# Two attention blocks on one core: where the first row maxima are split, when the k stacks are loaded, and where the reciprocals' spread stands in SP's queue

## Chip, core, metric

One NeuronCore of a Trainium2 chip. The metric is the device time of one execution in microseconds (us); before the change it is 1768.89, the median of three runs (1768.71 to 1769.63).

## What is computed

Two independent attention blocks over x of 2048 x 640 with 32 heads of 20, all in float32; their outputs stand side by side.

```python
# A: each position sees 8 keys, 2 apart
logits = einsum("bhsd,bhswd->bhsw", q, kg) * scale     # kg, vg: k, v at pos - 0, 2, .. 14
attn = softmax(where(mask, logits, -1e9)); o = einsum("bhsw,bhswd->bhsd", attn, vg)
# B: full attention
p = softmax(einsum("bhqd,bhkd->bhqk", q, k) * DH ** -0.5)
o = einsum("bhqk,bhkd->bhqd", p, v)
out = concat([oA @ woA, oB @ woB], axis=-1)            # q, k, v = x @ wqkv for both
```

## The kernel before, in words

Float32 factors are split into a high part that TensorE's fp32r can hold and the low rest, and a product is made of three passes (`PASSES`) or of stacked rows.

Stages: first A's projections, whose rows go to DRAM (`qa_d`, `ka_d`, `va_d`); then B's q and k projections, which go to DRAM as `qb_d` and `kb_d`; then B's v rows (30 groups of matmuls, `v_group`, `ve` to `vb_d`), beside which the row maxima of B's first 24 steps are made; then the main loop. Block A's attention runs all along on POOL (`a_scores`, `a_values`, tiles `akv`, `al`, `am`), a piece every few steps.

The main loop has `NS` = 512 steps. Heads go in 8 groups of 4 (`GH`); a group has 4 units, one for each 512 query columns (`NQC`), and a unit has 16 steps of 128 keys (`NKB`). `stacks[g]` holds the group's k (tile `bk`, loaded by `b_keys`, four transfers from `kb_d`, two buffers in turn) and v (`vb`, `v_piece`); `rings[0]` is the tile `bq` with the queries of four units. For a step PE makes four score tiles (`s_matmul`: rows of k against queries, 62 rows deep, `bq,bk` in the profile), ACT makes exp of each (`e`), and two steps later PE multiplies with v (`b_pv`, `e,vb`). 24 steps ahead (`LEAD`) PE makes the same products the other way round (`m_matmul`, 60 rows, `bk,bq`), and DVE reduces them to row maxima (`mx`).

The maximum enters the scores as two more rows of the query tile. `max_rows` does it once a unit: `turn` (DVE: last reduction and transpose into `mtr`), `parts` (split into a high and a low part), `store` (four DMAs `mdr<-mtr`), `load` (two DMAs `bq<-mdr`). The unit's first score matmul waits for the first of those loads.

`normalize` ends a unit: the sums, row `DH` of each head in `raw` (`braw`), go by DRAM into `sm` (`s_d<-braw`, `sm<-s_d`), `turn` takes their reciprocals on DVE and stores them (`s_d<-sm`), `bcast` spreads them over partitions (four DMAs `rb<-s_d`), POOL multiplies (`braw<-braw,rb`), and `out` stores `ot_b`.

What sets the order: every engine runs its instructions in the order in which the program names them (`InOrder`). `after(n, fn)` puts fn n steps ahead, `tick` runs what is due; a list of functions of one step runs in the order in which they were asked for. DVE work that must not stand anywhere is put in `beside` and comes at a mark `G` in the unit's table (`UNIT`, `UNIT_V`, `flush`). All loads and nearly all stores are issued by SP, whose queue is one line: an issue that has to wait holds up every later one. Each issue also waits for the landing of the DMA eight before it (eight semaphores in turn). The bank of the eight-bank tile `ps_st` is picked by `one` and `two` in the loop, before it by `bank` (0 to 3) and `wide` (pairs 4-5 and 6-7 in turn).

Of the kernel before, what the change touches and what calls it, by code (L numbers as in the profile page):

```python
# [9 lines left out]
F32 = mybir.dt.float32  # L10
F32R = mybir.dt.float32r
AF = mybir.ActivationFunctionType
ALU = mybir.AluOpType
# [10 lines left out]
NG = H // GH  # L24
# [16 lines left out]
NKB = 16  # L41
UP = 12
NS = NG * NQC * NKB
LEAD = 24
# [21 lines left out]
def attention_pair(ctx, tc, xa, wqk_a, wv_a, wo_a, xb, wqk_b, wv_b, wo_b, oa, ob):  # L66
# [6 lines left out]
    pe, gp, sp = (InOrder(tc, e) for e in (nc.tensor, nc.gpsimd, nc.sync))  # L73
    dve, act = InOrder(tc, nc.vector, 0.075, 960), InOrder(tc, nc.scalar, 0.111, 1400)


    now = [0]
    due = {}

    def after(n, fn, *args):  # L80
        due.setdefault(now[0] + n, []).append((fn, args))

    loop = [None]
    beside = []

    def small(us, op, *args):

        t = dve.us
        op(*args)
        dve.us = t + us  # L90
# [13 lines left out]
    def tick():  # L104
        now[0] += 1
        for fn, args in due.pop(now[0], ()):
            fn(*args)
# [93 lines left out]
    def x_pieces(x, n, second=None, at=()):  # L201

        t = columns(*at or (n,))
        src = x[:, n * 512:(n + 1) * 512].rearrange("(k p) c -> p k c", p=128)

        def piece(a, b):
            u = t[a // (KC - 1)]
            m = a % (KC - 1)
            split(u[:, 0, m:m + b - a], u[:, 1, m:m + b - a], src[:, a:b], "p", second)
        return t, [lambda a=a, b=b: piece(a, b) for a, b in PAIRS]  # L210
# [390 lines left out]
    def v_piece(g, b0, b1):  # L601

        sp.dma_start(stacks[g][1][:, b0:b1], vb_d[b0 * 128:b1 * 128, g * GH * VC:g * GH * VC + VG]
                     .rearrange("(b p) c -> p b c", p=128))
# [51 lines left out]
    def max_rows(m4, m1, q, qc):  # L656

        mt = sb.tile([128, 3, 32], F32R, tag="mtr", bufs=2, name="mtr")
        md = dr.tile([2, GH * 512], F32, tag="mdr", bufs=4, name="mdr")
        raw = mt[:, 0].bitcast(F32)  # L660

        def parts():
            gp.tensor_copy(mt[:, 1], raw)
            gp.tensor_tensor(mt[:, 2], raw, mt[:, 1].bitcast(F32), ALU.subtract)

        def store():
            for b in range(4):
                sp.dma_start(md.rearrange("t (j b c) -> b j t c", b=4, c=32)[b], mt[32 * b:32 * b + 16, 1:].bitcast(F32))

        def load():  # L670
            for r in range(2):
                sp.dma_start(q[r * HALF + BS:r * HALF + BM, qc].bitcast(F32),
                             md[:, r * 1024:(r + 1) * 1024].rearrange("t (p c) -> t p c", p=2))
        def turn():

            small(0.17, dve.tensor_reduce, m1[:, :16], m4.rearrange("p r a c -> p (r a) c"), AX.X, ALU.max)
            small(0.21, dve.transpose, raw, m1)
            after(1, parts)
            after(2, store)
            after(4, load)  # L680
        if loop[0] is None:
            after(1, turn)
        else:
            beside.append((turn,))

    def normalize(raw, g, c0, t, then):

        sm = sb.tile([128, 16], F32, tag="sm", bufs=2, name="sm")
        s_d = dr.tile([2, GH, 512], F32, tag="s_d", bufs=4, name="s_d")
        rb = sb.tile([128, 512], F32, tag="rb", bufs=2, name="rb")  # L690

        def bcast():
            for j in range(GH):
                sp.dma_start(rb[32 * j:32 * j + 32], s_d[1, j].partition_broadcast(32))

        def out():
            for j in range(GH):
                r0 = (g * GH + j) * DH
                sp.dma_start(ot_b[r0:r0 + DH, c0:c0 + 512], raw[32 * j:32 * j + DH])
        def turn():  # L700

            small(0.24, dve.reciprocal, sm, sm)
            after(1, sp.dma_start, s_d[1].rearrange("j (p c) -> j p c", c=16), sm)
            after(2, bcast)
            after(4, pool, raw, raw, rb, ALU.mult)
            after(8, out)
            if then:
                after(9, then)
        after(t, sp.dma_start, s_d[0], raw[DH:128:32])
        after(t + 1, sp.dma_start, sm, s_d[0].rearrange("j (p c) -> j p c", c=16))  # L710
        if now[0] - loop[0] < NS - LEAD - NKB // 2 - 4:
            after(t + 3, beside.append, (turn,))
        else:
            after(t + 3, turn)
# [32 lines left out]
    def b_max(i):  # L747

        m4 = max_tiles(i)[0]
        pq, ch = divmod(i % NKB, 2)  # L750
        for j in range(2):
            p = wide()
            for r in range(2):
                m_matmul(i, j, r, p[:, r])
            dve.tensor_reduce(m4[:, :, pq, 2 * ch + j], p, AX.X, ALU.max)
        max_end(i)
# [195 lines left out]
    def v_group(n, half, s):  # L952
        p = bank()
        rows15(p, lambda xi, k: chunk(XB[n], xi, k)[:, s % 4 * 128:s % 4 * 128 + 128], WV[half])
        ve = ones[s % 4]
        act.copy(ve[:, :16 * VC].rearrange("p (h c) -> p h c", c=VC)[:, :, :DH],
                 p[:, :320].rearrange("p (h d) -> p h d", d=DH))
        give(p)
        c = 16 * VC + 11 * half
        after(1, sp.dma_start, vb_d[s * 128:(s + 1) * 128, half * 16 * VC:half * 16 * VC + c], ve[:, :c])  # L960
# [29 lines left out]
    def a_load():  # L990

        w = big(2, [128, 2, KC, 320], "wx")
        wt[:] = [w]
        m = rows_a[0][1]
        return [lambda wi=wi, a=a, b=b: sp.dma_start(w[:, wi, a:b].bitcast(F32), wa_d[m, :, wi, a:b])
                for wi in range(2) for a, b in AK]
# [20 lines left out]
    for n, half, s in V_GROUPS[:-LAG]:  # L1017
        v_group(n, half, s)
        tick()
        groups += 1  # L1020
        if q_loads:
            for _ in range(4 if groups == 1 else 1):
                q_loads.pop(0)()
        if groups == 1:
            wait[0] = 5
        if groups in (8, 16):
            XB[groups // 8 - 1], more = x_pieces(xb, groups // 8 - 1, gp, (groups // 8 - 1, groups // 8 + 1))
            for fn in more:
                fn()
        if groups > 6:  # L1030
            for i in islice(steps, 1):
                b_max(i)
        if groups in (9, 11, 15, 17, 19, 23, 25, 28):
            next(a_work, None)
        if groups in (22, 23, 26):
            v_piece(0, *((8, 12), (12, 16), (0, 4))[(groups - 21) // 2])
        if groups in (18, 21):
            a_columns(UP + groups // 21)
        if groups == 24:
            for n, fn in enumerate(a_load()):  # L1040
                after(1 + n, fn)
        if groups == 14:
            a_turn(*done_a.pop(0)[1:])
        turn_parts()
        if groups == 28:
            wait[0] = 2
            load_out(wo_a, WO, (0,))
        if loads and groups >= 28:
            loads.pop(0)()
# [34 lines left out]
    next(steps)  # L1084
    for i in range(NS + LAG):
        g, sub = divmod(i, NQC * NKB)
        if sub == 4 and g + 1 < NG:
            for n, fn in enumerate(b_keys(g + 1)):
                after(1 + n, fn)
            after(33, v_piece, g + 1, 0, NKB)  # L1090
        if i >= NKB and i % NKB in (1, 3, 5, 7) and i // NKB + 3 < NG * NQC:
            b_queries(*divmod(i // NKB + 3, NQC))[i % NKB // 2]()
        if i in (NS - 56, NS - 40):
            out_first((i - NS + 56) // NKB)
        tick()
        if loads and i % 2:
            loads.pop(0)()
        if i > 14 and i % 4 == 3 and next(a_work, 0) == 0:
            for d in done_a:
                d[0] -= 1  # L1100
        if i % NKB == SLOT and done_a and done_a[0][0] <= 0:
            beside.append((lambda d=done_a.pop(0): a_turn(*d[1:]),))
        turn_parts()
        if i == 1:
            load_out(wo_a, WO, (1,))

            spare += [sb.tile([128, 2, 512], F32, tag="last0", bufs=2, name="more") for _ in range(2)]
        if i < NS - LEAD:
            next(steps, None)
            if not left_a[0] and not WO_b:  # L1110
                load_out(wo_b, WO_b)
            continue
        read_at.clear()
        flush()
        if i < NS:
            b_qk(i)
        if i % 2:
            b_pv(i - LAG - 1)
            b_pv(i - LAG)
            if fill:  # L1120
                fill.pop(0)()
# [57 lines left out]
```

## Time and profile before

| | |
|---|---|
| median of three runs | 1768.89 us |
| the profiled execution | 1771.62 us |
| its span, first to last instruction | 1769.8 us |
| busy: PE / DVE / ACT / POOL | 1751.3 / 1345.4 / 1333.0 / 1230.0 us |
| mean granted TensorE clock | 0.999 |
| 425 to 1420 us: busy PE / DVE / ACT / POOL | 986.5 / 951.2 / 915.2 / 864.6 of 995 us |

Rows of the timeline are: start, length in us, engine, line, operation, out<-in, shapes, count; in square brackets the idle time of that engine before it and what ended it. Nearly every row has line L61, that of the recording helper, so tiles tell the place. SPq rows are DMA issues, and their length is the issue, not the transfer. In the chain of waits a row "DMA x" starts at the issue and ends at the landing.

### The profile page before, as it was taken

To read this page: it belongs to the slowest core of one execution; us is meant where nothing else is said; L and a number is where in the kernel's file an instruction comes from. 1 tells how busy PE (TensorE), PEld (TensorE's weight loads), DVE (VectorE), ACT (ScalarE), POOL (GpSimd) and SP (SyncE) were. 2 spreads that over 40 slices of the span, in tenths; PEclk is the share of its full clock that TensorE was granted. 3 is DMA by queue.
4 is the path that set the end of the run, shared out by engine and by line. 5 is a ranking of instruction groups with operands and counts; after the bars stand their busy time and mean duration, and the time that the engine had idled before them with its cause. 6 is when DMAs were issued, how large, how long until landed. Compare 5 with 4: busy or idle time off the path is not lost.

```text
span 1769.8 us, 31997 instructions
## 1 busy us (share of the span) xinstructions
PE 1751.3 (99%) x11331; PEld 999.9 (56%) x11331; DVE 1345.4 (76%) x1819; ACT 1333.0 (75%) x2598; POOL 1230.0 (70%) x1088
## 2 busy tenths in 40 slices
PE   9999999999999999999999999999999999999999
PEld 8988888874454444444444444444444444444569
DVE  3102333679999999999999999999999999999400
ACT  4323222229989999999999999989999999989981
POOL 0000683585988888888989897988888898745442
PEclk9999999999999999999999999999999999999999
DMA  7657867774435554554464455535552534222123
GB/s 259 195 169 244 303 240 262 239 222 125 143 114 151 153 172 126 135 151 134 140 165 148 140 150 158 150 108 154 156 166 90 152 97 130 77 74 62 57 71 115
DMA packets 212152, 269.74 MB, mean 152 GB/s; under 512 B 91676, under 2 KB 131740, under 8 KB 211000
## 3 DMA queue, kind: packets, MB, share of 16 engines
q1 hardware_dynamic: 211416, 267.04, 50.3%
q8 instruction: 89, 1.46, 0.3%
q14 instruction: 71, 0.58, 0.1%
q10 hardware_dynamic: 576, 0.66, 0.1%
HBM read 192.87 MB, written 74.74 MB: 151 GB/s over the span
## 4 chain that ended last, share of the span: by engine, by line
PE 85%; DMA 4%; DVE 4%; POOL 3%; issue 1%; SPq 1%; ACT 1%; DVEq 0%; POOLq 0%; ACTq 0%
PE ps_st L61 85%; DVE mx L61 4%; DMA s_d<-sm 1%; POOL akv L61 1%; SPq L61 1%; DMA bq<-mdr 1%; ACT e L61 1%; DMA bq<-qb_d 1%; POOL xn L61 0%; DMA stg<-wv_b 0%; DMA mdr<-mtr 0%; DMA wx<-wa_d 0%; DMA qb_d<-pr 0%; POOL xl L61 0%; POOL ao L61 0%
## 5 line engine op out<-in xcount | busy, mean ns | idle before, releaser
L61 DVE TENSOR_REDUCE mx<-ps_st 128x1 f32<-128x512 f32 (+1 forms) x1500 | 1219.9, 879 | 83.2 <-PE ps_st L61 74.7
L61 ACT ACTIVATE e<-ps_st 128x512 f32<-128x512 f32 x2048 | 1067.9, 609 | 41.3 <-PE ps_st L61 22.7
L61 PE MATMUL ps_st<-bq,bk 62*128 62x512 f32 x2048 | 612.7, 441 | 6.7 <-DMA bq<-mdr 5.8
L61 PEld LDWEIGHTS ps_st<-bq,bk 62*128 62x128 f32 x2048 | 289.0, 184 | 486.1 <-ACT e L61 352.3
L61 PE MATMUL ps_st<-bk,bq 60*128 60x512 f32 x2048 | 556.2, 434 | 1.6 <-DMA bq<-qb_d 1.2
L61 PE MATMUL ps_st<-e,vb 128*32 128x512 f32 x4096 | 543.0, 604 | 3.1
L61 POOL TENSOR_TENSOR braw<-braw,more 128x512 f32<-128x512 f32 x224 | 288.1, 1286 | 171.1 <-ACT more L61 154.1
L61 POOL TENSOR_TENSOR akv<-akv,aq 128x1280 f32<-128x1280 f32 x64 | 188.5, 2945 | 184.8 <-DVE w L61 184.8
L61 POOL TENSOR_TENSOR akv<-akv 128x640 f32<-128x640 f32 (+3 forms) x304 | 282.6, 930 | 23.8
L61 PEld LDWEIGHTS ps_st<-bk,bq 60*128 60x128 f32 x2048 | 270.1, 184 | 31.5 <-DVE mx L61 10.5
L61 ACT COPY ro<-ps_st 128x320 f32<-128x320 f32 (+2 forms) x132 | 62.5, 475 | 191.8 <-PE ps_st L61 156.9
L61 PEld LDWEIGHTS ps_st<-e,vb 128*32 128x32 f32 x4096 | 82.2, 108 | 159.5 <-issue 73.6
L61 POOL TENSOR_TENSOR akv<-akv,al 128x1280 f32<-128x1280 f32 x64 | 152.1, 2376 | 0.2
L61 ACT COPY more<-ps_st 128x512 f32<-128x512 f32 x224 | 132.4, 591 | 1.6 <-PE ps_st L61 1.4
L61 PE MATMUL ps_st<-ww,xn 128*128 128x320 f32 x768 | 126.6, 315 | 0.0
L61 PEld LDWEIGHTS ps_st<-ww,xn 128*128 128x128 f32 x768 | 114.2, 189 | 20.0 <-ACT e L61 7.5
L61 PE MATMUL ps_st<-xn,w 128*128 128x512 f32 x480 | 117.6, 394 | 0.0
L61 PE MATMUL ps_st<-wc,xn 128*128 128x512 f32 (+1 forms) x432 | 102.0, 382 | 0.0
L61 PEld LDWEIGHTS ps_st<-xn,w 128*128 128x128 f32 x480 | 90.2, 188 | 20.9
L61 ACT CAST pr<-ps_st 128x512 fp32r<-128x512 f32 x40 | 23.5, 587 | 103.6 <-PE ps_st L61 103.6
L61 DVE TENSOR_TENSOR pr<-ps_st,pr 128x512 fp32r<-128x512 f32 x40 | 27.7, 692 | 93.0 <-ACT pr L61 93.0
L61 PEld LDWEIGHTS ps_st<-wc,xn 128*128 128x128 f32 x432 | 80.6, 190 | 13.9
(69 smaller groups left out, 1065.8 us busy)
## 6 DMA issues: line engine op xcount, KB each, us to landing
akv<-ka_d SPq DMA_DIRECT2D x128, 320.0 KB
akv<-va_d SPq DMA_DIRECT2D x128, 320.0 KB
wx<-wa_d SPq DMA_DIRECT2D x24, 480.0 KB
kb_d<-pr SPq DMA_DIRECT2D x20, 512.0 KB
qb_d<-pr SPq DMA_DIRECT2D x20, 512.0 KB
bk<-kb_d SPq DMA_DIRECT2D x16, 640.0 KB
bq<-qb_d SPq DMA_DIRECT2D x64, 160.0 KB
rb<-s_d SPq DMA_DIRECT2D x128, 64.0 KB
```

The costliest lines, as they stand in the source:

```text
L61: return self.tc.keep_in_program_order(op(*a, **k))
```

## The change

Three edits.

1. `parts` takes an engine. Before the loop (`loop[0] is None`, which holds for unit 0's maxima alone) VectorE splits at once, in the step of the transpose; the store comes one step later and the load two, where they were two and four. To this belongs that `wx`, block A's weights for the next rows (four loads, `a_load`), is asked for one step later.
2. In the loop, from group 1 on, the four `b_keys` loads of the next group are issued at steps 2 to 5 of the group and not at 4 to 7. The v piece stays at its step (35 from step 2, 33 from step 4).
3. In `normalize`, for units 0 to 28 (`slow`), `bcast` and the multiplication come one step later.

```diff
-        def parts():
-            gp.tensor_copy(mt[:, 1], raw)
-            gp.tensor_tensor(mt[:, 2], raw, mt[:, 1].bitcast(F32), ALU.subtract)
+        def parts(e=gp):
+            e.tensor_copy(mt[:, 1], raw)
+            e.tensor_tensor(mt[:, 2], raw, mt[:, 1].bitcast(F32), ALU.subtract)
...
             small(0.21, dve.transpose, raw, m1)
+            if loop[0] is None:
+                parts(dve)
+                after(1, store)
+                after(2, load)
+                return
             after(1, parts)
...
-            after(2, bcast)
-            after(4, pool, raw, raw, rb, ALU.mult)
+            after(2 + slow, bcast)
+            after(4 + slow, pool, raw, raw, rb, ALU.mult)
...
-        if now[0] - loop[0] < NS - LEAD - NKB // 2 - 4:
+        slow = now[0] - loop[0] < NS - LEAD - NKB // 2 - 4
+        if slow:
...
-                after(1 + n, fn)
+                after(2 + n, fn)
...
-        if sub == 4 and g + 1 < NG:
+        if sub == (2 if g else 4) and g + 1 < NG:
...
-            after(33, v_piece, g + 1, 0, NKB)
+            after(35 if g else 33, v_piece, g + 1, 0, NKB)
```

SP's queue at the first maxima (stage of the v rows; `stg`, `vb_d`, `vb`, `aq`, `akv` are other loads and stores), before:

```order
L61 DMA vb<-vb_d 128x4x95
L61 DMA vb_d<-ve 128x347
L61 DMA mdr<-mtr 16x2x32 x4
L61 DMA wx<-wa_d 128x960
L61 DMA vb_d<-ve 128x336
L61 DMA aq<-qa_d 128x640
L61 DMA akv<-ka_d 128x640 x2
L61 DMA wx<-wa_d 128x640
L61 DMA vb_d<-ve 128x336
L61 DMA vb<-vb_d 128x4x95
L61 DMA bq<-mdr 2x1024 x2
```

and now:

```order
L61 DMA vb<-vb_d 128x4x95
L61 DMA mdr<-mtr 16x2x32 x4
L61 DMA vb_d<-ve 128x347
L61 DMA bq<-mdr 2x1024 x2
L61 DMA vb_d<-ve 128x336
L61 DMA aq<-qa_d 128x640
L61 DMA akv<-ka_d 128x640 x2
L61 DMA wx<-wa_d 128x960
```

The maxima's store and load moved ahead of one v store, the first `wx` load, and the loads of block A; `wx` moved back.

SP's queue in the first unit of group 1 ( `bk` 40x4096 and 22x4096 are the two pieces of a half k stack), before:

```order
L61 DMA ot_b<-braw 20x512 x4
L61 DMA bq<-qb_d 40x1024
L61 DMA akv<-va_d 128x640 x2
L61 DMA s_d<-braw 4x512
L61 DMA ka_d<-ro 128x320
L61 DMA bk<-kb_d 40x4096
L61 DMA bq<-qb_d 20x1024
L61 DMA sm<-s_d 128x16
L61 DMA bk<-kb_d 22x4096
L61 DMA bk<-kb_d 40x4096
L61 DMA bq<-qb_d 40x1024
L61 DMA bk<-kb_d 22x4096
```

and now:

```order
L61 DMA ot_b<-braw 20x512 x4
L61 DMA bk<-kb_d 40x4096
L61 DMA bq<-qb_d 40x1024
L61 DMA bk<-kb_d 22x4096
L61 DMA akv<-va_d 128x640 x2
L61 DMA s_d<-braw 4x512
L61 DMA bk<-kb_d 40x4096
L61 DMA ka_d<-ro 128x320
L61 DMA bq<-qb_d 20x1024
L61 DMA sm<-s_d 128x16
L61 DMA bk<-kb_d 22x4096
L61 DMA bq<-qb_d 40x1024
```

Three of the four k loads now stand ahead of `ka_d<-ro` (a store that waits for ACT), and two ahead of the sums' store `s_d<-braw`.

SP's queue later in the same unit, at the reciprocals (`s_d<-sm` to the maxima's load), before:

```order
L61 DMA s_d<-sm 128x16
L61 DMA rb<-s_d 32x512 x4
L61 DMA mdr<-mtr 16x2x32 x4
L61 DMA akv<-ka_d 128x640 x2
L61 DMA bq<-mdr 2x1024 x2
```

and now:

```order
L61 DMA s_d<-sm 128x16
L61 DMA mdr<-mtr 16x2x32 x4
L61 DMA akv<-ka_d 128x640 x2
L61 DMA rb<-s_d 32x512 x4
L61 DMA bq<-mdr 2x1024 x2
```

The spread, which reads what `s_d<-sm` wrote, changed places with the maxima's store and two loads of block A; it still stands ahead of `bq<-mdr`. On POOL the multiplication keeps its place but in units 27 and 28, where it falls behind one and two splits.

## The prediction

> **What bounds the kernel now.** I began with the page's first line, then asked who waits for whom on PE.
>
> ```profile
> PE 1751.3 (99%) x11331; PEld 999.9 (56%) x11331; DVE 1345.4 (76%) x1819; ACT 1333.0 (75%) x2598; POOL 1230.0 (70%) x1088
> ...
> PE ps_st L61 <- DMA bq<-mdr: 5.8, 6, 1.9
> ```
>
> PE works 1751.3 of 1769.8 us, so only what it waits for, or what slows it, can be won. Of its waits the largest by far is for the maxima's load into the query tile: 5.8 us in six places. PE's timeline shows them, the idle time in brackets.
>
> ```profile
> 391.40 0.46 PE L61 MATMUL ps_st<-bq,bk 62*128 62x512 f32 x1 [1.92 <-DMA bq<-mdr]
> ...
> 603.02 0.50 PE L61 MATMUL ps_st<-bq,bk 62*128 62x512 f32 x1 [1.10 <-DMA bq<-mdr]
> ...
> 768.45 0.49 PE L61 MATMUL ps_st<-bq,bk 62*128 62x512 f32 x1 [0.49 <-DMA bq<-mdr]
> ...
> 933.94 0.49 PE L61 MATMUL ps_st<-bq,bk 62*128 62x512 f32 x1 [0.47 <-DMA bq<-mdr]
> ...
> 1100.04 0.50 PE L61 MATMUL ps_st<-bq,bk 62*128 62x512 f32 x1 [1.06 <-DMA bq<-mdr]
> ...
> 1265.96 0.50 PE L61 MATMUL ps_st<-bq,bk 62*128 62x512 f32 x1 [0.81 <-DMA bq<-mdr]
> ```
>
> The first is at the loop's start. The other five are some 166 us apart, one a group: the first score of the second unit of groups 1 to 5. Together they are 1.10 + 0.49 + 0.47 + 1.06 + 0.81 = 3.93 us.
>
> Is such a hole given back, because ACT and DVE catch up in it? ACT's copy of the first partial sum comes once a unit; its rows at the starts of units 4 to 7:
>
> ```profile
> 568.25 0.59 ACT L61 COPY braw<-ps_st 128x512 f32<-128x512 f32 x1
> ...
> 610.74 0.59 ACT L61 COPY braw<-ps_st 128x512 f32<-128x512 f32 x1
> 651.83 0.59 ACT L61 COPY braw<-ps_st 128x512 f32<-128x512 f32 x1
> 693.20 0.59 ACT L61 COPY braw<-ps_st 128x512 f32<-128x512 f32 x1
> ```
>
> The stretch with the 1.10 us hole takes 42.49 us, the next 41.09, the one after 41.37. Against the latter it is 1.12 us longer. So a hole costs its whole length.
>
> The hole at 391.40 has a second price. Windows of PE around it, the granted clock in the column PEclk:
>
> ```profile
> core 0: us, PE busy (x) PEld busy (x) DVE busy (x) ACT busy (x) POOL busy (x), PEclk, DMA share, GB/s
> 389.47:392.89 3.42, 1.50 (x11) 1.28 (x10) 2.86 (x3) 1.02 (x2) 3.34 (x2) 1.00 1.06 377
> 392.89:396.30 3.41, 3.41 (x16) 2.88 (x14) 0.16 (x1) 0.62 (x2) 1.60 (x2) 0.50 0.97 319
> ```
>
> Behind the window in which PE was busy for 1.50 of 3.42 us, the clock stood at half for 3.41 us, with PE busy all the time: at most 1.7 us lost. The five later holes, up to 1.10 us, cost no clock; the window that holds them says
>
> ```profile
> 425.00:1420.00 995.00, 986.50 (x6874) 468.94 (x6866) 951.21 (x1311) 915.15 (x1794) 864.63 (x756) 1.00 0.50 143
> ```
>
> **Edit 1, the first maxima.** What stood between the transpose and the store:
>
> ```profile
> 367.50 0.21 DVE L61 STREAM_TRANSPOSE mtr<-mx 128x32 f32<-128x32 f32 x1
> 367.94 2.36 DVE L61 TENSOR_REDUCE mx<-ps_st 128x2 f32<-128x1024 f32 x2 [0.22 <-PE ps_st L61]
> ...
> 379.43 0.21 POOL L61 CAST mtr<-mtr 128x32 fp32r<-128x32 f32 x1
> ...
> 380.00 1.73 SPq L61 DMA_DIRECT2D mdr<-mtr  x4
> ...
> 385.72 5.54 DMA bq<-mdr
> ```
>
> The transpose ends at 367.71, POOL comes to the split only at 379.43, the store goes at 380.00, and the load takes from 385.72 to 391.26. Now DVE splits at about 367.7. No row has these two operations on DVE; the transpose of the same size takes 0.21 us, so 0.4 us for both. DVE was idle for 0.22 us there anyway, waiting for PE, so 0 to 0.2 us of delay, once; I take 0. POOL is rid of two short instructions, off the path. On SP the store then goes a step after the transpose and the load the step after that; with steps of some 3 us the load is issued before 377 (an estimate) and lands, even with 5.54 us, before 383. What is late next? The program gives the answer: the score matmul that waited goes into bank 0, but the maxima matmul right behind it takes bank 7, half of the pair that the last reductions before the loop read.
>
> ```profile
> 389.28 2.36 DVE L61 TENSOR_REDUCE mx<-ps_st 128x2 f32<-128x1024 f32 x2 [0.70 <-PE ps_st L61]
> ```
>
> These are two reductions; the first, of pair 6-7, ends at 390.46. So the maxima matmul starts at some 390.6 instead of 391.40: **0.8 us**, not 1.92, and a hole of some 0.7 us remains (score until 389.95, then nothing). Since holes of 1.10 us cost no clock, the half clock goes. What it costs is seen in the twelve matmuls of a v group in it and in the next group:
>
> ```profile
> 391.83 2.72 PE L61 MATMUL ps_st<-ww,xn 128*128 128x320 f32 x12
> ...
> 396.62 2.03 PE L61 MATMUL ps_st<-ww,xn 128*128 128x320 f32 x12
> ```
>
> 0.69 us there, and the rest of the 3.41 us at half speed besides: between 0.69 and 1.7, I take **1.5 us**, near the upper end, since PE had work throughout. The `wx` loads go a step later in the program, but SP no longer stands until 380 for the split, so in time they go no later than before; they are wanted only in the loop's fourth step, and were one late, PE would stand there, ahead of block A's first rows, by as long. Edit 1: 2.3 us.
>
> [...]
>
> **Edits 2 and 3, the five holes.** SP's rows of group 1's first unit:
>
> ```profile
> 561.02 1.46 SPq L61 DMA_DIRECT2D ot_b<-braw  x4
> ...
> 572.76 0.31 SPq L61 DMA_DIRECT2D bk<-kb_d  x1
> ...
> 573.56 0.34 SPq L61 DMA_DIRECT2D sm<-s_d  x1
> ...
> 579.95 0.87 SPq L61 DMA_DIRECT2D akv<-ka_d  x2
> ...
> 594.76 2.15 SPq L61 DMA_DIRECT2D rb<-s_d  x4
> 597.03 1.74 SPq L61 DMA_DIRECT2D mdr<-mtr  x4
> ...
> 600.13 0.56 SPq L61 DMA_DIRECT2D bq<-mdr  x2
> ```
>
> and in the chain of waits of the same place:
>
> ```profile
> 589.20 5.50 DMA s_d<-sm
> 598.35 1.69 DMA mdr<-mtr
> 600.13 2.85 DMA bq<-mdr
> ```
>
> The store of the reciprocals, a small one, takes 5.50 us, because the k stacks and loads behind them still move; the spread waits for it; and the maxima's store, though long ready, stands behind the spread. It lands 600.13 + 2.85 = 602.98, PE wanted it at 603.02 - 1.10 = 601.92.
>
> Edit 3 alone: the maxima's store goes at 589.6, right behind `s_d<-sm`, ends by 591.4, two loads follow (0.8), the spread still waits until 594.7 and takes 2.15 us, the load goes at 596.9 and lands by 599.8, which is 2.1 us ahead of PE. If all landings were as slow as the reciprocals' 5.50, it would be 602.4, half a us late. Edit 2 alone: three of four k loads go ahead of `ka_d<-ro`. They wait for the last scores of the group before, near 603.0 - 42.5 = 560.5, so the first may go at 562.5, behind the `ot_b` stores, 10 us sooner than 572.76. That wait for PE is new at this place; behind it on SP stand a query load, two `akv` loads and `s_d<-braw`, none wanted within the next ten us, and at 562.5 it should be over already. The backlog ends sooner, and `s_d<-sm` lands faster. In units without k loads it lands at once:
>
> ```profile
> 548.05 0.38 SPq L61 DMA_DIRECT2D s_d<-sm  x1
> 549.55 1.71 SPq L61 DMA_DIRECT2D rb<-s_d  x4
> ```
>
> 1.5 us. With both edits the load lands between 597 and 599.8. So the five holes go whole: **3.93 us**. Next late there are ACT and DVE at the pace of the units without a hole, 41.4 us, which is in the sum already.
>
> What the spread's new place costs: in units like that at 548.05 it goes behind the maxima's store (1.7 us, as at 597.03) and up to three more issues (0.3 to 0.4 each), so up to 3 us later, and POOL's multiplication with it by 0 to 3 us; behind it on POOL stand adds of partial sums, on which ACT's copies depend only four copies later. What stands behind the spread on SP is the maxima's load, which then waits for the landing of `s_d<-sm` as before. POOL works 864.63 of 995 us, so it is idle for 130 us, over 5 a unit, and that hides it; nothing on PE waits for the product before the last groups. I take 0; without that cover each unit would hold ACT up by as much. In units 27 and 28 the multiplication falls behind splits on POOL, still ahead of its store: 0.
>
> The sum: 0.8 + 1.5 + 3.93 = **6.2 us**. The profiled execution of 1771.62 (span 1769.8) would be 1765.4; the runs' median lies 2.7 lower, at 1768.89, and the same 6.2 off it gives **1762.7**.
>
> **Rivals.** *The half clock has another cause than the hole, or the hole of 0.7 us that remains brings it too*: 1.5 less, 1764.2. For it: it is seen only once. Against it: the five holes without it. 8%. [...]
>
> *Edit 1 wins all of its hole* (the maxima matmul finds its bank free): 1.92 + 1.7 + 3.93 = 7.5, 1761.4. Against it: DVE's row at 389.28. 7%.
>
> *The k stacks, sooner, fill the queue at another place, and the five holes stay or move*: the maxima's load of the next unit, the `akv` loads or the sums' way meet the backlog from 562 on. Then only edit 1 counts: 1766.6. For it: the loads are no smaller. Against: edit 3 alone has 2 us to spare. 8%.
>
> *Slower: DVE stands for the sums.* `s_d<-braw` now goes behind two k loads and `sm<-s_d` behind a third. Reciprocals have a fixed place on DVE, ahead of the reductions on which PE's banks hang:
>
> ```profile
> 587.26 0.24 DVE L61 RECIPROCAL sm<-sm 128x16 f32<-128x16 f32 x1
> ```
>
> `sm<-s_d` was issued at 573.56 and had 13.7 us. One k load of 640 KB takes some 7.2 us (572.76 to 579.95, where the issue eight places on was let go). The small ones are of 352 KB:
>
> ```profile
> bk<-kb_d SPq DMA_DIRECT2D x2, 640.0 KB
> ...
> bk<-kb_d SPq DMA_DIRECT2D x2, 352.0 KB
> ```
>
> so 7.2 x 352 / 640 = 4.0 us by size. From 562.5 all four take 2 x 7.2 + 2 x 4.0 = 22.4 us, to 585, if they run one behind another; the sums stand behind three of them, so near 581, with the `akv` loads between somewhat later. That leaves 2 to 6 us. From a landing at 587.3 on, each us late stops DVE and then PE by as much, in each of six groups; with 1.7 us late the gain is 6 x 1.7 = 10.2 less and the kernel slower by 4: 1773. 6%. *An edit does nothing at all* (the five holes and the first stay for a reason not seen): 1768.9, 3%.
>
> **How the numbers follow.** The forecast 1762.7 with bounds 1761.4 to 1764.2 has 68%; with the two neighbours that end on these bounds, 83%. The range goes on to 1766.0 for holes that close only in part, and down to 1760.9. About 0.2%, 3.5 us, can be told from no change here. Faster by more needs a time under 1765.3: the first three cases, 83%. Within 0.2%: the case with edit 1 alone (8%), no effect (3%), 11%. Slower: the sums' case, 6%.
>
> **What would show it.** PE's waits for `bq<-mdr` gone or under 1 us in all; no window of half clock between 385 and 400, and a hole of 0.7 us near 390, ended by DVE; `s_d<-sm` in the units with k loads landing in 2 to 4 us; their stretch between ACT's copies at 41.4 us; the unchanged units at 41.1 and 41.4. Wrong: a DVE wait for `sm<-s_d` in the loop, PE waits for `bq<-mdr` in other units, or longer units without a hole.

## The result and the profile after

The changed kernel takes 1765.7 us (median of 20 runs, 1764.89 to 1768.37) against 1769.16 of the kernel before (20 runs, 1766.18 to 1774.36). The ratio is 0.9983, with a 95% interval of 0.9977 to 0.9989: 3.0 us faster, between 1.9 and 4.1. Forecast were 6.2. The median lies inside the forecast's bounds, which go up to 1766.0 for holes that close only in part, but that is luck: here they close whole, and the time is missing at another place.

The profiled execution alone tells something else. It took 1765.34 us (forecast: 1765.4), its span is 1763.5, so it is 6.3 us shorter than the profiled execution of before. PE's whole list of waits in it, behind the two of before that the prediction did not show:

```profile
PE ps_st L61 <- DMA bq<-qb_d: 1.2, 2, 0.6
PE ps_st L61 <- DVE mx L61: 0.6, 1, 0.6
```

and now:

```profile
PE ps_st L61 <- DVE mx L61: 2.4, 4, 0.9
PE ps_st L61 <- POOL ident L61: 1.4, 1, 1.4
PE ps_st L61 <- DMA vb_d<-ve: 0.4, 1, 0.4
```

The load `bq<-mdr`, 5.8 us before, is gone from it. Its waits for DVE, one of 0.6 us before, are now 2.4. ACT's copies of the first partial sum, units 4 to 7:

```profile
566.34 0.59 ACT L61 COPY braw<-ps_st 128x512 f32<-128x512 f32 x1
607.72 0.59 ACT L61 COPY braw<-ps_st 128x512 f32<-128x512 f32 x1
648.82 0.59 ACT L61 COPY braw<-ps_st 128x512 f32<-128x512 f32 x1
690.21 0.59 ACT L61 COPY braw<-ps_st 128x512 f32<-128x512 f32 x1
```

41.38, 41.10 and 41.39 us, where the first was 42.49: the hole of the second unit is closed, and its whole length came back. The first copy comes 1.91 us sooner than in the execution of before (568.25), so this much was won by then, and the rest of the 6.3 behind it.

That two profiles gave 6.3 where 6.2 was forecast is luck in part. From the start of the loop's first v group (391.83 before, 391.35 now) to the score matmul behind the last wait for DVE (1653.51 and 1647.35) the kernel now needs 1256.00 us in place of 1261.68, which is 5.7 less: the five holes, 3.93, and 1.75 more, which fits the half clock. Ahead of that v group only 0.5 is won, not 0.8, and there the changed execution also lacked 1.2 us of waits for query loads (`bq<-qb_d`, near 318), which no edit is about, and had 0.4 of another wait.

SP's rows in group 1's first unit:

```profile
560.68 0.28 SPq L61 DMA_DIRECT2D bk<-kb_d  x1
...
587.29 0.38 SPq L61 DMA_DIRECT2D s_d<-sm  x1
587.76 1.82 SPq L61 DMA_DIRECT2D mdr<-mtr  x4
589.63 0.90 SPq L61 DMA_DIRECT2D akv<-ka_d  x2
590.62 1.76 SPq L61 DMA_DIRECT2D rb<-s_d  x4
592.82 0.52 SPq L61 DMA_DIRECT2D bq<-mdr  x2
```

The maxima's load goes at 592.82 instead of 600.13. The spread at 590.62 no longer waits.

At the first maxima the trace shows a price that the forecast did not have. The columns are start, length, engine, operation; POOL's rows stand beside DVE's:

```profile
366.61 0.21 DVE L61 STREAM_TRANSPOSE mtr<-mx 128x32 f32<-128x32 f32 x1
366.68 1.29 POOL L61 TENSOR_TENSOR xl<-stg,xl 128x512 fp32r<-128x512 f32 x1
366.85 1.16 DVE L61 CAST mtr<-mtr 128x32 fp32r<-128x32 f32 x1
367.92 0.72 POOL L61 CAST aot<-back 128x640 fp32r<-128x640 f32 x1
368.05 0.64 DVE L61 TENSOR_TENSOR mtr<-mtr 128x32 fp32r<-128x32 f32 x1
368.61 2.34 DVE L61 TENSOR_REDUCE mx<-ps_st 128x2 f32<-128x1024 f32 x2
...
369.87 0.49 PE L61 MATMUL ps_st<-bk,bq 60*128 60x512 f32 x2 [0.28 <-DVE mx L61]
...
371.00 0.50 PE L61 MATMUL ps_st<-bk,bq 60*128 60x512 f32 x2 [0.64 <-DVE mx L61]
```

The split takes DVE 1.80 us, not 0.4. The cast ends at 368.01, POOL's subtraction at 367.97; DVE's subtraction ends at 368.69, POOL's cast at 368.64. The reductions behind it are late, and PE stands for 0.28 and 0.64 us. The hole at the loop's start is there as forecast, behind the score and ended by DVE, 0.86 us where 0.7 was written, and the clock stays full (1.00 in the windows from 386.06 to 399.71):

```profile
390.92 0.49 PE L61 MATMUL ps_st<-bk,bq 60*128 60x512 f32 x1 [0.86 <-DVE mx L61]
```

So the question is a double one: why do the runs show half of what the two profiles show, and what do the edits give one by one?

### The profile page after: what moved, and what is told of

Its sections match the earlier page's. It is cut to its first block, busy times and chain, and to the rows that moved or that the text cites. A ratio compares the mean times of both kernels' runs of the same rounds, so it can differ in the third digit from the quotient of the medians.

```text
span 1763.5 us, 31971 instructions
## 1 busy us (share of the span) xinstructions
PE 1749.7 (99%) x11331; PEld 998.7 (57%) x11331; DVE 1346.4 (76%) x1821; ACT 1333.1 (76%) x2598; POOL 1229.7 (70%) x1086
## 4 chain that ended last, share of the span: by engine, by line
PE 88%; DVE 6%; POOL 2%; DMA 1%; issue 1%; ACT 1%; SPq 0%; DVEq 0%; POOLq 0%; ACTq 0%
PE ps_st L61 88%; DVE mx L61 6%; POOL akv L61 1%; DMA bk<-kb_d 1%; ACT e L61 1%; POOL xn L61 0%; DMA vb_d<-ve 0%; SPq L61 0%; POOL ww L61 0%; POOL braw L61 0%; DMA stg<-xa 0%; POOL ao L61 0%; DMA rb<-s_d 0%; POOL xl L61 0%; POOL aot L61 0%
```

## The experiments

Theories. *Slow draw*: the sum was made against one execution that had longer holes and a half clock that others do not have. *Split*: the VectorE split waits for POOL and eats the gain of the first edit. Rivals: the holes are the same in every execution and the gain is lost elsewhere; the split's instructions are slow by themselves.

### The kernel before, once more

No edit.

> The kernel before, unchanged, for the spread of its executions and for a second profile. Theory 'slow draw': the one profiled execution (1771.62) was slower than most, its holes and its half clock larger than usual; the executions spread over 1766 to 1774, some with a mean clock of 0.999 or less and some of 1.000, and the new profile shows other hole lengths or no half clock. Rival 'fixed': a second profile shows the same six holes (1.92, 1.10, 0.49, 0.47, 1.06, 0.81, each within 0.1) and the same half clock; then the shortfall is not in the kernel before.

It took 1769.8 us (ratio 1.0001, 0.9992 to 1.0009). Its profiled execution took 1767.52, 4.1 us less than the first one, with a mean granted TensorE clock of 1.000. PE at the loop's start, and two windows of the clock there. (In the clock records of three executions the full clock lasts whole multiples of 3.413 us: 385.71 us in the first execution are 113 of them, 1757.86 in the changed kernel's 515, 1761.28 in this one 516. So windows are laid on these borders, counted from the record of each execution.)

```profile
389.51 0.46 PE L61 MATMUL ps_st<-bq,bk 62*128 62x512 f32 x1 [1.36 <-DMA bq<-mdr]
```

```profile
386.49:389.90 3.41, 2.05 (x13) 1.25 (x12) 2.71 (x3) 0.43 (x1) 3.33 (x4) 1.00 1.06 387
389.90:393.31 3.41, 3.41 (x23) 2.87 (x21) 1.42 (x3) 1.42 (x3) 3.18 (x3) 1.00 1.01 356
```

The hole is 1.36 us and not 1.92, and no half clock follows (1.00 in the column behind POOL's). The five later holes are 0.57, 0.73, 0.58, 0.14 and 0.87, 2.9 us in all and not 3.93, each of another length than before. The rival "fixed" falls: neither the holes nor the half clock are the same from one execution to the next.

The mean clock of every run gives a rough count. It was under 1.000 in 26 of the 33 runs of the kernel before that stand beside this series, whose median is 1769.66; the 7 others have 1767.70. In the 11 runs of this experiment, the same kernel, it was so in 5. Of the changed kernel's 20 runs three were under 1.000. A half clock at any place counts in that mean, and so does one at the very end, as in the first execution (0.50 from 1768.50 to 1769.80, with no engine busy).

### Edit 1 alone

```diff
+            if loop[0] is None:
+                parts(dve)
+                after(1, store)
+                after(2, load)
+                return
...
-                after(1 + n, fn)
+                after(2 + n, fn)
```

> Edit 1 alone (VectorE splits the first maxima, wx a step later). Theory 'clock': the half clock behind the first hole comes in every execution of before; edit 1 alone gains 0.8 + 1.5 less the 0.9 that the slow split costs, 1.4 us. Rival 'clock by chance': the half clock comes in few executions of before, and edit 1 alone gains 0 to 0.5 us, with a hole of 0.86 near 391 ended by DVE in its profile. In both the five later holes stay, 3 to 4 us in all.

1769.26 us, ratio 1.0003 (0.9994 to 1.0011): nothing gained, within 1.1 us faster and 1.9 slower, as the rival "clock by chance" said; the 1.4 us of the other theory lie outside. The trace has the split's holes (0.25 and 0.64), the 0.86 at 390.38, and four later holes of 3.1 us in all. Its profiled execution also shows, 1250 us later and where the kernel was not changed, what looks like the same thing. DVE and POOL at 1643, and PE behind them:

```profile
1643.11 1.55 POOL L61 TENSOR_TENSOR ww<-stg,ww 128x640 fp32r<-128x640 f32 x1
1643.16 2.05 DVE L61 TENSOR_TENSOR xl<-stg,xl 128x512 fp32r<-128x512 f32 x1
...
1645.86 0.70 PE L61 MATMUL ps_st<-bk,bq 60*128 60x512 f32 x1 [1.20 <-DVE mx L61]
```

```profile
1642.58:1645.99 3.41, 2.20 (x10) 0.99 (x10) 3.37 (x4) 3.41 (x8) 3.33 (x3) 1.00 0.10 33
1645.99:1649.40 3.41, 3.41 (x15) 1.09 (x15) 2.30 (x4) 0.29 (x2) 1.60 (x3) 0.50 0.05 7
```

DVE's subtraction, one of eleven of its kind with a median of 0.69 us, took 2.05 beside POOL's; PE stood for 1.20 us, and a half clock followed. In that unit, not in the split, this execution lost up to 2.9 us (1.20, and at most half of 3.41).

### Edit 2 alone, edit 3 alone, both

```diff
-        if sub == 4 and g + 1 < NG:
+        if sub == (2 if g else 4) and g + 1 < NG:
...
-            after(33, v_piece, g + 1, 0, NKB)
+            after(35 if g else 33, v_piece, g + 1, 0, NKB)
```

> Edit 2 alone (k stacks two steps sooner). If the five holes cost 3.9 us in most executions: 3.5 to 4 us faster, with the reciprocals' store landing in 2 us instead of 5.5 and no wait of PE for the maxima's load but the first. If the holes are smaller in most executions than in the profiled one: 1 to 2.5 us faster, with the same profile.

1765.24 us, ratio 0.9977 (0.9968 to 0.9987): 4.1 us faster, between 2.3 and 5.7. That is nearer to the branch in which the holes cost 3.9 us in most executions than to that of smaller holes. All five are gone; SP's rows:

```profile
587.37 0.38 SPq L61 DMA_DIRECT2D s_d<-sm  x1
588.92 1.71 SPq L61 DMA_DIRECT2D rb<-s_d  x4
...
595.21 0.56 SPq L61 DMA_DIRECT2D bq<-mdr  x2
```

The spread follows the reciprocals' store after 1.55 us, which was 5.56 before.

```diff
-            after(2, bcast)
-            after(4, pool, raw, raw, rb, ALU.mult)
+            after(2 + slow, bcast)
+            after(4 + slow, pool, raw, raw, rb, ALU.mult)
```

> Edit 3 alone (the spread behind the maxima's store). The reciprocals' store still lands after 5 us, but the maxima's load should land 2 us ahead of PE: the five holes go, and the time is that of edit 2 alone within 0.5 us. If the load's landing is slowed as well by what is still moving, holes of some 0.5 us stay and the gain is half of edit 2's.

1767.08 us, ratio 0.9994 (0.9977 to 1.0011): by time not to be told from no change, and 1.8 us above edit 2's median, where at most 0.5 was expected. The trace is clearer: the five holes are gone (PE waits for `bq<-mdr` once only, at the loop's start), and SP's last row comes near the forecast for this edit alone, 596.9:

```profile
588.64 0.38 SPq L61 DMA_DIRECT2D s_d<-sm  x1
...
594.10 2.47 SPq L61 DMA_DIRECT2D rb<-s_d  x4
596.67 0.53 SPq L61 DMA_DIRECT2D bq<-mdr  x2
```

Nine of its 12 runs had a mean clock under 1.000; the three others have a median of 1764.49, edit 2's seven such runs 1765.21. So its shortfall seems to lie in the runs of lower clock. Its profiled execution had the longest first hole, with the half clock behind it:

```profile
388.15:391.56 3.41, 1.19 (x9) 0.67 (x6) 2.70 (x3) 0.74 (x2) 3.33 (x2) 1.00 1.07 386
391.56:394.97 3.41, 3.41 (x14) 3.15 (x12) 0.35 (x1) 0.28 (x1) 1.89 (x2) 0.50 0.95 306
```

Both edits together, without edit 1 (the two diffs above):

> Edits 2 and 3 together, the first maxima as before. If edit 1 nets nothing (its slow split gives back what its earlier load wins), this is as fast as all three edits: 3 to 4 us faster than before, no wait of PE for the maxima's load but the first, of 1.3 to 2.2 us, and a half clock behind it in part of the executions. If edit 1 has a worth of its own beside the others, this is 1 us or more slower than all three.

1765.35 us, ratio 0.9977 (0.9965 to 0.9989). That is no slower than all three edits (0.9983, 0.9977 to 0.9989): edit 1 has no worth that can be measured beside them, though an interval of 2.1 us on either side is wide. First hole 1.77 us, no half clock in this execution, which is the same 1763 in span as that with all three (1763.0 and 1763.5).

### What the split costs by itself

Twelve more pairs of the split's two DVE instructions on a scratch tile, six at steps of block A's projections and six in the stage of the v rows:

```diff
+    def pair_on_dve():
+        dve.tensor_copy(sc[:, 1], sc[:, 0].bitcast(F32))
+        dve.tensor_tensor(sc[:, 2], sc[:, 0].bitcast(F32), sc[:, 1].bitcast(F32), ALU.subtract)
```

> All three edits with twelve more pairs of the split's two DVE instructions (128x32) on a scratch tile: six in block A's projections, where POOL is idle, six in the stage of the v rows, where POOL works. Theory 'VectorE waits for POOL': with POOL idle the two take 0.1 to 0.25 us each; with POOL at work they end where a POOL instruction ends, up to 2 us. Rival 'slow by themselves': 1.1 and 0.6 us in both places. Its output is the reference's; its time is longer by what the pairs hold up.

A pair with POOL idle (the changed kernel's profile has no POOL row between 60 and 100 us):

```profile
72.58 0.18 DVE L61 CAST scr<-scr 128x32 fp32r<-128x32 f32 x1
72.79 0.19 DVE L61 TENSOR_TENSOR scr<-scr 128x32 fp32r<-128x32 f32 x1
```

and one beside POOL's work on block A:

```profile
349.48 0.73 POOL L61 TENSOR_TENSOR al<-al,am 128x256 f32<-128x256 f32 x1
349.50 0.76 DVE L61 CAST scr<-scr 128x32 fp32r<-128x32 f32 x1
350.17 2.95 POOL L61 TENSOR_TENSOR akv<-akv,aq 128x1280 f32<-128x1280 f32 x1
350.29 2.88 DVE L61 TENSOR_TENSOR scr<-scr 128x32 fp32r<-128x32 f32 x1
```

Of the twelve casts and the twelve subtractions the median took 0.18 and 0.19 us, the longest 1.73 and 2.88. In the rows beside POOL's the cast ends at 350.26 and the subtraction at 353.17, each 0.05 us after POOL's instruction (350.21 and 353.12); for the split in the changed kernel it was 0.04 and 0.05. So the instructions are not slow by themselves: these four ended with POOL's, as if they waited for it. By what they are held no row tells. The one run of this kernel took 1771.03 us, with PE's waits for DVE at 6.4 us in place of 2.4.

### Two versions that use this

POOL splits, but in the transpose's step:

```diff
-                parts(dve)
+                parts()
```

> All three edits, but the first maxima are split by POOL, in the step of the transpose. Theory 'VectorE waits for POOL': the two holes of 0.28 and 0.64 us near 370 go, POOL comes to the split some 6 us sooner than before, the load still lands long ahead of 389, and the time is 0.9 us under that of the three edits. Rival 'the holes are another's': they stay near 370 and the time is that of the three edits.

1764.37 us, ratio 0.9970 (0.9958 to 0.9982), 1.3 us under the median of the three edits, where 0.9 was expected; the intervals overlap. The holes near 370 are gone; the only ones left in PE's list against DVE are 0.86 at 388.64 and 0.63 at the end. POOL's and SP's rows:

```profile
371.91 0.21 POOL L61 CAST mtr<-mtr 128x32 fp32r<-128x32 f32 x1
372.20 0.25 POOL L61 TENSOR_TENSOR mtr<-mtr 128x32 fp32r<-128x32 f32 x1
...
372.48 1.73 SPq L61 DMA_DIRECT2D mdr<-mtr  x4
```

And with it the bank planner's state at the loop's start:

```diff
-    read_at += 8 * [0.0]
+    read_at += 4 * [0.0] + [2.2, 2.2, 1.0, 1.0]
```

> As the kernel with POOL's early split, and the bank planner is told that the four wide banks are still being read when the loop starts, so that the first maxima matmul takes a free bank. If the hole of 0.86 us near 391 is the wait for DVE's reading of bank 7, it goes: 0.86 us faster than with POOL's early split alone, 1.8 us faster than the three edits. If the next matmuls meet the same wait, the hole only moves and nothing is won.

1763.52 us, ratio 0.9963 (0.9951 to 0.9975): 6.5 us faster than before, the fastest of all. PE goes from the stage before into the loop without a hole:

```profile
388.98 0.73 PE L61 MATMUL ps_st<-bk,bq 60*128 60x512 f32 x4
389.55 0.39 PE L61 MATMUL ps_st<-bq,bk 62*128 62x512 f32 x1
389.55 0.39 PE L61 MATMUL ps_st<-bk,bq 60*128 60x512 f32 x1
389.87 2.03 PE L61 MATMUL ps_st<-ww,xn 128*128 128x320 f32 x12
```

Its interval and that of all three edits do not overlap. It does overlap with that of POOL's early split alone: the 0.9 us expected of the bank (0.85 between the medians) is shown by the hole that is gone, not by time. Its own profiled execution is not the best one (1762.8 us in span, POOL's early split alone 1761.5): it waited 1.4 us for query loads at 318, and once 0.32 at 1271.

## Why the prediction was wrong

**The bound and the five holes: right in kind.** PE is the bound (before, it was busy for 1751.3 of 1769.8 us), a hole costs its length (without the 1.10 us the stretch of 42.49 took 41.38, 1.11 less), and edits 2 and 3 close all five; either alone does, as the forecast had it for edit 3. No wait of DVE for the sums came in the changed kernel's loop, so the rival on the slow side fell. **Their size was read from one draw.** The step "together they are 3.93 us" holds for one execution. Two others of kernels that have them show 2.9 and 3.1; the three give 3.3. The runs cannot tell these apart: edit 2 alone won 4.1, between 2.3 and 5.7.

**Edit 1 is the step that failed: 2.3 us were forecast, and alone it measures zero.** It failed in two terms. "The first maxima" had 0.8 us from the hole, with 0 to 0.2 for the split. The split costs two holes of 0.9 us together instead, since its two instructions ended with POOL's and took 1.16 and 0.64 us, where a pair with POOL idle took 0.18 and 0.19. And 1.92 us of hole were nothing unusual: it was 1.36, 1.66, 2.22 and 1.77 in the four other profiles without edit 1, 1.79 on average. What edit 1 leaves is 0.86 + 0.92 = 1.78. When PE starts the loop's first v group shows it too: at 391.83, 389.94, 390.71, 391.11 and 390.50 us in the five profiles without edit 1 (mean 390.8), at 390.80 with edit 1 alone and 391.35 with all three.

**The half clock, 1.5 us, was counted as if it came always.** Its size was about right: from the first v group to the score matmul behind the last wait for DVE, edit 3 alone, with the half clock, took 1257.83 us, and edits 2 and 3 together, without it, 1256.10, which is 1.7 less. But it followed the first hole in two of the five profiles without edit 1 (holes of 1.92 and 2.22), not in the others (1.36, 1.66, 1.77). So what its end is worth on average is near 0.6 us, 1.5 x 2/5, an estimate from five executions. With edit 1 the holes are 0.86 us and less, and the half clock was not behind them in either profile.

**The sum was taken off the wrong time.** 6.2 us come from an execution of 1771.62, 2.7 above the median, and were taken off the median. That part of those 2.7 came from its longer holes and its half clock, and so could not be won from the median as well, is argued and not measured. With 3.3 for the holes, 0 for edit 1's holes and up to 0.6 for the clock it is 3.3 to 3.9, within the measured 1.9 to 4.1.

PE's busy time in a window does not tell by itself when the clock halves: windows of 3.41 us with 1.50 us of it (the first execution) and 1.19 (edit 3 alone) were followed by half the clock, one with 2.05 (the kernel before, once more) was not, and one with 2.20 (edit 1 alone) was.

What stays open: how much of the 2 us between runs of full and of lower mean clock is the first hole's half clock, and how much falls at other places, as at 1646 in one execution. The counts do not follow the first hole alone: the two kernels with edit 2 but without edit 1 keep that hole, and of their 20 runs 6 had a mean clock under 1.000, against 9 of 12 with edit 3 alone and 31 of the 44 runs of before (20 of 29 in the later series). Why edit 2 goes with fewer no trace here tells, since only one execution of each experiment was traced. And edit 3's worth alone was not measured to better than 3.0 us on either side.

## What to carry to other kernels

A wait that hangs on DMA landings had another length in each execution here (1.36 to 2.22 us for one and the same): take its size from several profiles, or set the sum against an execution near the median, before it is taken off the median. Before small work moves to VectorE, look at what GpSimd runs at that moment: here a 128x32 cast and subtraction, 0.18 and 0.19 us with GpSimd idle, ended 0.04 to 0.05 us after GpSimd's instruction and took up to 2.88 us, and in the changed kernel the reductions behind them came late (holes of 0.28 and 0.64 us on PE). When a wait at a stage's start is removed, look for the next one in the program's buffers; here it was a bank (0.86 us), named in the prediction, and one line at the planner took it away.

## What was not expected of the hardware

- VectorE's 128x32 cast and subtraction took 0.18 and 0.19 us with GpSimd idle, and up to 1.73 and 2.88 us over the twelve pairs; in the rows shown beside GpSimd's they ended 0.04 to 0.05 us after its instruction. At the kernel's end a 128x512 subtraction of 0.69 us took 2.05 beside one of GpSimd, in the profile of edit 1 alone; it ended 0.55 us after it.
- TensorE's clock was halved for 3.41 us behind single holes: one of 1.92 and one of 2.22 us at the loop's start, but also one of 1.20 us (the window before it had PE busy for 2.20 of 3.41 us), while holes of 1.36, 1.66 and 1.77 us passed without. Part of it goes with where the hole lies against the windows' borders: those of 1.92 and 2.22 us fell whole into one window (PE busy for 1.50 and 1.19 us), those of 1.66 (edit 2 alone) and 1.77 (edits 2 and 3) were parted by a border (at 389.66 and 388.82), which left PE busy for 2.38 and 2.15 us in the emptier window. The holes of 1.20 us, with the half clock, and of 1.36, without (PE busy for 2.05 us), each lay whole in one window, so what decides between these two is open.
